# Linear attention, a dense and a sparse mixture of experts in one kernel: a new order for the first unit of tokens, its loads on two queues, small inputs loaded later

## The chip, the cores and the metric

The kernel runs on one core of a Trainium2 chip. The metric is the device time of one execution in microseconds, the median of several runs. A core has TensorE (matmuls, with a separate stream of weight loads), VectorE, ScalarE, GpSimd, and SyncE (SP), which here only issues DMAs. Each engine executes its own instructions in program order and waits on semaphores for the others. DMAs are issued from queues; in this kernel SP's is the main one, ScalarE has one as well. The profile calls the engines PE (PEld for its weight loads), DVE, ACT, POOL and SP.

## The reference

Three parts follow each other. The first is a gated linear attention over 2 batches, 8 heads, 768 tokens and 48 channels per head; the second is a dense mixture of 4 experts on the 1,536 rows of 384 channels, weighted by normalised `domain_probs`; the third a noisy top-2 mixture of 8 experts.

```python
for t in range(S):
    state = alpha[:, :, t, :, None] * state + einsum('bhd,bhe->bhde', k[:, :, t], v[:, :, t])
    y[:, :, t] = einsum('bhd,bhde->bhe', q[:, :, t], state)
...
p = domain_probs / (domain_probs.sum(-1, keepdims=True) + 1e-09)
for e in range(E):
    h = np.maximum(x @ w1[e], 0.0)
    out += p[:, e:e + 1] * (h @ w2[e])
```

The third part takes logits from two small matrices (`w_gate`, `w_noise`) and an input `noise`, and sends each row through its two best experts.

## The kernel before

The attention works on units of 128 or 256 tokens (`sizes`); the first unit has 128. A unit is cut into groups of two blocks, a block being a pair of heads by 128 tokens; the first unit has two groups (k=0 and k=1 in the plan), the second, of 256 tokens, four (k=2 to 5). Each group goes through stages: `decays` (alpha is transposed on TensorE into a "tr" bank; VectorE takes running products forward, A, and backward, F, and a reciprocal `rc`), `keys` (k transposed, VectorE multiplies it by F to K; ScalarE scales it to G), `queries` (q transposed, times A, is Q), `scores` (G by Q on TensorE into banks sc0 and sc1; VectorE masks them to M), `keys_back` (K transposed back, copied by ScalarE to Kn), `states` (Kn by v into sc0; VectorE writes or updates the states S), and `outputs` (S by Q and M by v into sc1; ScalarE copies them to `xn`). At the end of a unit `back` transposes `xn`; ScalarE writes `xh` (for the first unit `x32` ahead of it), VectorE the remainder `xl`.

`plan()` gives every stage of every group a step; `stream()` walks the steps, and inside a step goes by a fixed order of stages. `busy(n)` puts n dummy matmuls of 512 columns ahead of a stage, by the table `IDLE`; fourteen more stand at the start of the program. Every stage takes its bank for dummies from the four "g" banks, whether n is 0 or not. The schedule is manual: what is written first is issued first on each engine.

When `rows_at[0]` steps are done, the first expert of the dense mixture starts on the first 128 tokens: `hidden` for one column of 128 hidden channels at a time (the matmuls of line 475, six records each, into a "g" bank; ScalarE writes `hh`, VectorE `hl`), then the products. `drive` deals its twelve steps out over the steps of the attention that go on beside it, up to the end of the second unit, and ahead of each `W.step` may prepare a piece of weights (line 142 on ScalarE: the four pieces of the first expert's second matrix, numbers 0 to 3; numbers 4 to 7 are its first matrix and are first used as they are).

On SP's queue stand, in this order: the first unit in two halves of the heads (alpha, k, q each, 96 KB), its v, and then, of the second unit and the weights, `"a", "k", "q", 4, 0, 5, "v", 1, 6, 2, 7, 3`. ScalarE's queue has the small inputs `prob`, `noise` and the two halves of `wgn`, which arrive in rows of 16 or 32 bytes. A row of the attention's inputs has 48 numbers, 192 bytes; a unit of 128 tokens has 1,024 rows for each of the four inputs. A first-matrix piece has 384 rows of 1 KB, a second-matrix piece 256 rows of 1.5 KB. Four short operations of VectorE (lines 553 to 556) normalise `prob` ahead of everything else; it is first used in line 521, when the first products are done.

Of the kernel before, what the change touches and what calls it, by code (L numbers as in the profile page):

```python
# [10 lines left out]
F32 = mybir.dt.float32  # L11
# [6 lines left out]
OP = mybir.AluOpType  # L18
AX = mybir.AxisListType

P = 128
# [7 lines left out]
def kernel(  # L29
# [16 lines left out]
    nc = tc.nc  # L46
    B, H, S, D = q.shape
    N, DM = out.shape
    E1, _, FF = moe_w1.shape
    E2 = moe2_w1.shape[0]  # L50
    NB = N // P
# [6 lines left out]
    BM = UM // P  # L58
    KD = DM // P
    KF = FF // P  # L60
    HP = H // 2
# [5 lines left out]
    const = ctx.enter_context(tc.tile_pool(name="const", bufs=1))  # L67
# [5 lines left out]
    def ps(tag, bufs=1):  # L73
        return psum.tile([P, 512], F32, tag=tag, name=tag, bufs=bufs)
# [111 lines left out]
    def busy(n):  # L186

        t = ps("g", 4)
        for _ in range(n):
            nc.tensor.matmul(t.rearrange("x (c i) -> x c i", c=4), ones_b, ones_b[:, None, :].to_broadcast([P, 4, P]),  # L190
                             start=True, stop=True)
# [21 lines left out]
    apool = att.enter_context(tc.tile_pool(name="apool", bufs=1))  # L213
# [4 lines left out]
    for nm, n in (("a", 2), ("k", 1), ("q", 1)):  # L218
        for i in range(n):
            t = apool.tile([P, BM, H, 64], F32, name=f"x_{nm}{i}", tag=f"x_{nm}{i}")  # L220
# [8 lines left out]
    V = {}  # L229

    def inputs(nm, u):
        if nm == "a":
            return X[nm, u % 2]
        return X[nm, 0] if u else early[:, "kq".index(nm)]

    def load_unit(u, names, p0=0, p1=HP):

        if u >= NU:
            return
        b, h0 = divmod(starts[u], S)  # L240
        hs = slice(2 * p0, 2 * p1)
        for nm in names:
            if nm == "v":
                V[u] = apool.tile([P, BM, H, D], F32, tag="v", name="v", bufs=2)
            for c in range(sizes[u] // P):
                frm = src[nm][b, hs, h0 + c * P:h0 + (c + 1) * P, :].rearrange("h p d -> p h d")
                if nm == "v":
                    nc.sync.dma_start(V[u][:, c, hs], frm)
                    continue
                nc.sync.dma_start(inputs(nm, u)[:, c, hs, :D], frm)  # L250


    prob = const.tile([P, NB, E1], F32, name="prob")
    nc.scalar.dma_start(prob, moe_domain_probs.rearrange("(b p) e -> p b e", p=P))
    noise = const.tile([P, NB, E2], F32, name="noise")
    nc.scalar.dma_start(noise, moe2_noise.rearrange("(b p) e -> p b e", p=P))
    wgn = const.tile([P, KD, 2 * E2], F32, name="wgn")
    nc.scalar.dma_start(wgn[:, :, :E2], moe2_w_gate.rearrange("(c p) e -> p c e", p=P))
    nc.scalar.dma_start(wgn[:, :, E2:], moe2_w_noise.rearrange("(c p) e -> p c e", p=P))

    W = Weights()

# [2 lines left out]
    for i in range(2):  # L265
        t = apool.tile([P, UM], F32, name=f"suffix{i}")
# [3 lines left out]
    for p in range(HP):  # L270
        t = apool.tile([P, BM + 1, 2 * D], F32, name=f"S{p}")
# [6 lines left out]
    def attention(u):  # L278

        b, h0 = divmod(starts[u], S)  # L280
# [6 lines left out]
        def slot(c):  # L287
            return (starts[u] // P + c) % (BM + 1)

        def at(i):  # L290
            return slice(i * P, (i + 1) * P)

        def transposed(nm, g):
            t = ps("tr", 2)
            for i, (p, c) in enumerate(groups[g]):
                nc.tensor.transpose(t[:, at(i)], inputs(nm, u)[:, c, 2 * p:2 * p + 2, :].rearrange("x h d -> x (h d)"), ident)  # L296
            return t[:, :UM]
# [19 lines left out]
        def keys(g):  # L317
            A, K, Q, G, rc = st[g]
            nc.vector.tensor_mul(K, transposed("k", g), st[g, "F"])
            for i in range(BM):  # L320
                nc.scalar.activation(G[:, at(i)], K[:, at(i)], AF.Copy, scale=rc[:, i:i + 1])

        def queries(g):
            A, K, Q, G, rc = st[g]
            nc.vector.tensor_mul(Q, transposed("q", g), A)
# [15 lines left out]

        def scores(g):
            A, K, Q, G, rc = st[g]
            t = [ps("sc0"), ps("sc1")]
            for i in range(BM):
                for j in range(2):
                    rows = slice(64 * j, 64 * j + D)
                    nc.tensor.matmul(t[j][:, at(i)], G[rows, at(i)], Q[rows, at(i)], start=True, stop=True)  # L348
            for j in range(2):
                M = apool.tile([P, BM, P], F32, tag=f"M{j}", name="M")  # L350
                nc.vector.tensor_mul(M, t[j][:, :UM].rearrange("x (c i) -> x c i", c=BM),
                                     tri[:, None, :].to_broadcast([P, BM, P]))
                st[g, j] = M

# [22 lines left out]

        def outputs(g):
            A, K, Q, G, rc = st[g]
            t = ps("sc1")  # L380
            for i, (p, c) in enumerate(groups[g]):
                inter = not (first and c == 0)
                if inter:
                    nc.tensor.matmul(t[:, i * 2 * D:(i + 1) * 2 * D], Q[:, at(i)], St[p][:, slot(c), :],  # L384
                                     start=True, stop=False)
                for j in range(2):
                    o = i * 2 * D + j * D
                    nc.tensor.matmul(t[:, o:o + D], st[g, j][:, i, :], V[u][:, c, 2 * p + j, :], start=not inter,  # L388
                                     stop=not inter or j == 1)
            if g == 0:  # L390
                st["xn"] = apool.tile([P, BM, DM], F32, tag="xn", name="xn")
            xn = st["xn"]
            p = groups[g][0][0]
            n = 2 * D * BM // UB
            nc.scalar.activation(xn[:, :UB, 2 * p * D:2 * p * D + n],
                                 t[:, :UB * n].rearrange("x (c d) -> x c d", c=UB), AF.Copy)

        def loads(g, names, v):
            p0, p1 = groups[g][0][0], groups[g][-1][0] + 1
            if p1 % 2 == 0:  # L400
                load_unit(v, names, p1 - 2, p1)
# [22 lines left out]
        def outputs_(g):  # L424
            outputs(g)
            if g == len(groups) - 1:
                load_unit(u + 2, "v")

        return len(groups), UB, (outputs_, states, keys, scores, keys_back, queries_, decays_), back

    suffixes = itertools.cycle(suffix)

    rows_at = {}
    NEAR = 2

    IDLE = {(2, 0): 5, (1, 0): 5, (2, 1): 2, (1, 1): 4, (2, 2): 4, (1, 2): 2, (0, 0): 1, (0, 1): 1, (0, 2): 1}

    def plan():
        at = {}
        base = 0  # L440
        k = 0
        for u in range(NU):
            n, UB, stages, back = attention(u)
            for g in range(n):
                near = k < NEAR
                for order, (stage, off) in enumerate(zip(stages, (5, 4, 1, 3, 3, 2, 0) if near else (7, 6, 1, 5, 3, 2, 0))):
                    at.setdefault(base + off, []).append((order, k, stage, g))
                end = base + (5 if near else 7)
                base += 2 if near else 3
                k += 1  # L450
            for c in range(UB):
                at.setdefault(end + 1 + c, []).append((-1, k, back, c))
            rows_at[u] = end + 1 + UB
        return at

    steps = plan()

    def stream():
        for i in range(max(steps) + 1):
            for order, k, f, g in sorted(steps.get(i, ()), key=lambda z: z[:2]):  # L460
                busy(IDLE.get((order, k), 0))
                f(g)
            yield

# [84 lines left out]
                pass  # L549


    psm = const.tile([P, NB], F32, name="psm")
    nc.vector.reduce_sum(psm, prob, axis=AX.X)
    nc.vector.tensor_scalar(psm, psm, 1e-9, None, op0=OP.add)
    nc.vector.reciprocal(psm, psm)
    nc.vector.tensor_mul(prob, prob, psm[:, :, None].to_broadcast([P, NB, E1]))

    for i in range(2):
        load_unit(0, "akq", i * HP // 2, (i + 1) * HP // 2)
    load_unit(0, "v")  # L560
    for what in ("a", "k", "q", 4, 0, 5, "v", 1, 6, 2, 7, 3):
        if type(what) is int:
            W.fetch(what)
        else:
            load_unit(1, what)
    W.n_raw = 2 * NG
    rows_now = stream()
    now = 0

    def until(i):  # L570
        nonlocal now
        while now < i:
            now += 1
            next(rows_now, None)
            yield

    for _ in until(rows_at[0]):
        if now >= 15 and W.n_prep < 4:
            W.prep()

    def n_moe(n):
        return KF + n // P * (KF // 2)
# [11 lines left out]
    hst = ExitStack()  # L594
    hidden_in.append((hst.enter_context(tc.tile_pool(name="hpool", bufs=1, side="right")), 4 * P))


    NS = E2 * SB
    BL = 3
# [554 lines left out]
```

## Time and profile before

| | us |
|---|---|
| median of 3 runs | 765.06 (764.93 to 765.39) |
| the profiled execution, its own time | 764.46 |
| its span, first to last instruction | 762.7 |
| TensorE busy | 750.6 |
| VectorE busy | 351.4 |
| ScalarE busy | 246.0 |
| GpSimd busy | 160.6 |

The span is what the trace covers; the execution's own time is a little longer. Busy time counts an engine's instructions; what it waited for, and since when, is in the rows further down. Each row of a timeline merges equal instructions that follow each other: start, length, engine, line, operation, output and inputs, shape, how many, and in brackets how long the engine was idle before it and whose semaphore ended that.

### The profile page before, as it was taken

What the parts mean: (1) busy time and instruction counts of PE and PEld (TensorE: products, weight loads), DVE (VectorE), ACT (ScalarE), POOL (GpSimd) and SP (SyncE); (2) the same over time, 40 slices, a digit from 0 to 9 for tenths busy, and PEclk for the clock granted to TensorE, in tenths of its full rate; (3) what the DMA queues carried; (4) which work ended last, traced back from release to release, by engine and by line L of the source; (5) the groups of instructions that cost most, each with busy time, mean ns of one, the idle gap of its engine ahead of it and who ended that gap; (6) DMA issues with size and microseconds to landing.
All of it is one profiled execution on the core that took longest, in us unless ns stands there. A gap on an engine that the chain in (4) does not pass through costs nothing.

```text
span 762.7 us, 11958 instructions
## 1 busy us (share of the span) xinstructions
PE 750.6 (98%) x4658; PEld 707.6 (93%) x4658; DVE 351.4 (46%) x864; ACT 246.0 (32%) x481; POOL 160.6 (21%) x174
## 2 busy tenths in 40 slices
PE   9999999999999999999999999999999999999996
PEld 5899999999998989899899999989999999999996
DVE  5877566663222131222212346366745554654641
ACT  2643322232311031211223323333525444444430
POOL 2520000001510023100124100011352424424331
PEclk9999999999999999999999999999999999999999
DMA  9836212100620012100023300011763554654710
GB/s 187 221 75 125 52 32 43 22 1 8 209 75 1 0 42 83 43 0 1 22 63 103 94 21 12 32 42 29 220 206 122 186 161 148 212 161 136 228 63 32
DMA packets 97998, 66.97 MB, mean 88 GB/s; under 512 B 57577, under 2 KB 94500, under 8 KB 97936
## 3 DMA queue, kind: packets, MB, share of 16 engines
q1 hardware_dynamic: 89008, 51.92, 24.6%
q0 software_dynamic: 5024, 14.13, 5.8%
q8 instruction: 39, 0.64, 0.4%
q10 hardware_dynamic: 3904, 0.10, 0.4%
q14 instruction: 23, 0.19, 0.1%
HBM read 56.69 MB, written 9.82 MB: 87 GB/s over the span
## 4 chain that ended last, share of the span: by engine, by line
PE 93%; DVE 5%; ACT 1%; issue 0%; POOL 0%; POOLq 0%; DVEq 0%
PE g L480 13%; PE g L479 13%; PE g L481 13%; PE g L494 10%; PE g L496 10%; PE g L495 10%; PE g L994 3%; PE g L996 3%; PE g L995 3%; PE sc L388 2%; PE tr L296 2%; PE sc L348 2%; PE tr L927 1%; PE sc L362 1%; PE sc L384 1%; PE g L190 1%
## 5 line engine op out<-in xcount | busy, mean ns | idle before, releaser
L485 ACT ACTIVATE hh<-g 128x384 fp32r<-128x384 f32 (+8 forms) x200 | 96.9, 485 | 281.2 <-PE g L481 261.6
L486 DVE SCALAR_TENSOR_TENSOR hl<-g,hh 128x384 fp32r<-128x384 f32 (+8 forms) x200 | 109.5, 550 | 159.5 <-ACT hh L485 154.1
L494 PE MATMUL g<-w2h,hl 128*128 128x384 f32 x464 | 161.7, 348 | 0.0
L496 PE MATMUL g<-w2h,hh 128*128 128x384 f32 x464 | 156.5, 337 | 0.0
L495 PE MATMUL g<-w2l,hh 128*128 128x384 f32 x464 | 156.4, 337 | 0.0
L479 PE MATMUL g<-xh,w1l 128*128 128x512 f32 (+2 forms) x360 | 127.0, 353 | 0.0
L480 PE MATMUL g<-xl,w1h 128*128 128x512 f32 (+2 forms) x360 | 124.4, 346 | 0.0
L481 PE MATMUL g<-xh,w1h 128*128 128x512 f32 (+2 forms) x360 | 124.3, 345 | 0.0
L143 POOL TENSOR_TENSOR w1l<-raw,w1h 128x768 fp32r<-128x768 f32 x16 | 29.3, 1841 | 280.2 <-ACT w1h L142 280.2
L494 PEld LDWEIGHTS g<-w2h,hl 128*128 128x128 f32 x464 | 87.3, 188 | 0.5
L495 PEld LDWEIGHTS g<-w2l,hh 128*128 128x128 f32 x464 | 87.4, 188 | 0.3
L496 PEld LDWEIGHTS g<-w2h,hh 128*128 128x128 f32 x464 | 87.2, 188 | 0.0
L523 DVE SCALAR_TENSOR_TENSOR acc<-g,prob,acc 128x384 f32<-128x384 f32 x36 | 22.2, 618 | 119.7 <-PE g L496 119.7
L480 PEld LDWEIGHTS g<-xl,w1h 128*128 128x128 f32 x360 | 67.8, 188 | 6.3 <-DVE xl L413 0.3
L481 PEld LDWEIGHTS g<-xh,w1h 128*128 128x128 f32 x360 | 67.7, 188 | 6.3
L479 PEld LDWEIGHTS g<-xh,w1l 128*128 128x128 f32 x360 | 67.8, 188 | 6.0
L479 PE MATMUL g<-xth,w1l 128*128 128x256 f32 (+6 forms) x216 | 73.2, 339 | 0.0
L480 PE MATMUL g<-xtl,w1h 128*128 128x256 f32 (+6 forms) x216 | 71.4, 331 | 0.1
L481 PE MATMUL g<-xth,w1h 128*128 128x256 f32 (+6 forms) x216 | 71.3, 330 | 0.0
L142 ACT ACTIVATE w2h<-raw 128x768 fp32r<-128x768 f32 x44 | 36.4, 843 | 35.3 <-issue 23.0
L945 POOL DMA_INDIRECT out_dram<-yo,si_c x26 | 26.1, 1004 | 87.1 <-DVE yo L944 80.9
L994 PE MATMUL g<-hh,w2l 128*128 128x432 f32 (+4 forms) x120 | 43.3, 361 | 0.0
(193 smaller groups left out, 1056.1 us busy)
## 6 DMA issues: line engine op xcount, KB each, us to landing
raw<-in_moe_w_dram SPq DMA_DIRECT2D x92, 384.0 KB, 4.3
v<-in_v_dram SPq DMA_DIRECT2D x12, 192.0 KB, 2.9
out_dram<-zero SPq DMA_DIRECT2D x1, 2304.0 KB
x2d<-acc SPq DMA_DIRECT2D x12, 192.0 KB, 4.5
x_a<-in_alpha_dram SPq DMA_DIRECT2D x20, 96.0 KB, 2.1
x_k<-in_k_dram SPq DMA_DIRECT2D x18, 96.0 KB, 2.6
x_q<-in_q_dram SPq DMA_DIRECT2D x18, 96.0 KB, 2.7
acc<-in_moe_w_dram SPq DMA_DIRECT2D x4, 384.0 KB, 7.1
```

The costliest lines, as they stand in the source:

```text
L142: nc.scalar.activation(hi, r, AF.Copy)
L143: (nc.gpsimd if e < E1 or own else nc.vector).tensor_sub(lo, r, hi.bitcast(F32))
L479: nc.tensor.matmul(t[:, :n], wl, hx[:, kd, t0:t0 + n], start=(kd == 0), stop=False)
L480: nc.tensor.matmul(t[:, :n], wh, lx[:, kd, t0:t0 + n], start=False, stop=False)
L481: nc.tensor.matmul(t[:, :n], wh, hx[:, kd, t0:t0 + n], start=False, stop=(kd == KD - 1))
L485: nc.scalar.activation(hh[:, :n], t[:, :n], AF.Relu)
L486: nc.vector.scalar_tensor_tensor(hl[:, :n], t[:, :n], 0.0, hh.bitcast(F32)[:, :n], op0=OP.max, op1=OP.subtract)
L494: nc.tensor.matmul(t[:m, :DM], hl[:, o:o + m], wh, start=(f == 0), stop=False)
L495: nc.tensor.matmul(t[:m, :DM], hh[:, o:o + m], wl, start=False, stop=False)
L496: nc.tensor.matmul(t[:m, :DM], hh[:, o:o + m], wh, start=False, stop=(f == KF - 1))
L945: nc.gpsimd.indirect_dma_start(out=parts_of_out[s], out_offset=bass.IndirectOffsetOnAxis(ap=SLOT[e * SB + s][2][:n, e * SB + s:e * SB + s ...
L994: nc.tensor.matmul(t[:, :n], wl, hh[:, :n], start=(f == 0), stop=False)
```

## The change

The first unit gets step tables of its own. All of its transposes of alpha, k and q come first, then both scores, both outputs, `back`, both `keys_back` and both `states`; its rows are ready after step 6 instead of 8, so the expert starts two steps sooner, with the first unit's `states` still to come. From the third group on every stage keeps its step. Two transposes, the second group's scores and its outputs take "g" banks, masks have two buffers each. The dummies are dealt out anew. The first unit's k and q are issued from ScalarE's queue; `prob` follows weight piece 1 on SP's queue, `noise` and `wgn` come on SP's queue after the attention. The normalising of `prob` stands behind step 6. The condition `now >= 15` that goes was never true there.

```diff
-    def load_unit(u, names, p0=0, p1=HP):
+    def load_unit(u, names, p0=0, p1=HP, queue=nc.sync):
...
+    for i in range(2):
+        load_unit(0, "a", i * HP // 2, (i + 1) * HP // 2)
+        load_unit(0, "kq", i * HP // 2, (i + 1) * HP // 2, nc.scalar)
+    load_unit(0, "v")
...
-            t = ps("tr", 2)
+            t = ps("g", 4) if u == 0 and (nm, g) in (("q", 0), ("a", 1)) else ps("tr", 2)
...
-            t = [ps("sc0"), ps("sc1")]
+            t = [ps("g", 4), ps("g", 4)] if u == 0 and g else [ps("sc0"), ps("sc1")]
...
-                M = apool.tile([P, BM, P], F32, tag=f"M{j}", name="M")
+                M = apool.tile([P, BM, P], F32, tag=f"M{j}", name="M", bufs=2)
...
-            t = ps("sc1")
+            t = ps("g", 4) if u == 0 and g else ps("sc1")
...
-    NEAR = 2
-
-    IDLE = {(2, 0): 5, (1, 0): 5, (2, 1): 2, (1, 1): 4, (2, 2): 4, (1, 2): 2, (0, 0): 1, (0, 1): 1, (0, 2): 1}
+    NEAR = ({"decays": 0, "keys": 0, "queries": 0, "scores": 2, "outputs": 4, "keys_back": 6, "states": 7},
+            {"decays": 0, "keys": 1, "queries": 1, "scores": 3, "outputs": 5, "keys_back": 6, "states": 8})
+    FAR = {"decays": 0, "keys": 1, "queries": 2, "keys_back": 3, "scores": 5, "states": 6, "outputs": 7}
+    ORDER = ("outputs", "states", "keys", "scores", "keys_back", "queries", "decays")
+
+    IDLE = {("scores", 0): 5, ("scores", 1): 6, ("outputs", 0): 2, ("outputs", 1): 1, ("back", 1): 2}
...
-    psm = const.tile([P, NB], F32, name="psm")
-    nc.vector.reduce_sum(psm, prob, axis=AX.X)
-    nc.vector.tensor_scalar(psm, psm, 1e-9, None, op0=OP.add)
-    nc.vector.reciprocal(psm, psm)
-    nc.vector.tensor_mul(prob, prob, psm[:, :, None].to_broadcast([P, NB, E1]))
-
-    for i in range(2):
-        load_unit(0, "akq", i * HP // 2, (i + 1) * HP // 2)
-    load_unit(0, "v")
-    for what in ("a", "k", "q", 4, 0, 5, "v", 1, 6, 2, 7, 3):
+    for what in ("a", "k", 4, "q", 5, "v", 6, 7, 0, 1, "p", 2, 3):
         if type(what) is int:
             W.fetch(what)
+        elif what == "p":
+            nc.sync.dma_start(prob, moe_domain_probs.rearrange("(b p) e -> p b e", p=P))
...
     for _ in until(rows_at[0]):
-        if now >= 15 and W.n_prep < 4:
-            W.prep()
+        pass
+
+    psm = const.tile([P, NB], F32, name="psm")
+    nc.vector.reduce_sum(psm, prob, axis=AX.X)
+    nc.vector.tensor_scalar(psm, psm, 1e-9, None, op0=OP.add)
+    nc.vector.reciprocal(psm, psm)
+    nc.vector.tensor_mul(prob, prob, psm[:, :, None].to_broadcast([P, NB, E1]))
```

In `plan()` the groups of `NEAR` take their steps from these tables, and inside a step the first group's keys and queries come behind the other stages, followed by the second group's decays.

## Rows read from the trace of the kernel before

**Rows 1.** The page, TensorE's busy time, share of the span, instructions.

```profile
PE 750.6 (98%) x4658; PEld 707.6 (93%) x4658; DVE 351.4 (46%) x864; ACT 246.0 (32%) x481; POOL 160.6 (21%) x174
```

**Rows 2.** Windows: busy time by engine, granted clock, DMA share, GB/s.

```profile
5.00:30.00 25.00, 23.56 (x176) 17.58 (x175) 18.50 (x63) 10.98 (x29) 6.22 (x4) 1.00 1.01 234
30.00:40.00 10.00, 10.00 (x88) 9.35 (x87) 8.44 (x29) 5.27 (x14) 4.64 (x3) 1.00 0.74 157
```

**Rows 3.** Timeline of TensorE, 0 to 30 us.

```profile
1.13 4.90 PE L190 MATMUL g<-ones_b 128*128 128x512 bf16 x14 [1.13 <-DVE ones_b L185]
5.86 0.38 PE L296 MATMUL tr<-ident,x_a 128*128 128x128 f32 x2
...
9.31 0.72 PE L348 MATMUL sc<-Q,G 48*128 48x128 f32 x8
...
20.23 0.94 PE L475 MATMUL g<-acc,raw 128*128 128x128 f32 x6 [0.34 <-ACT acc L411]
...
29.00 0.69 PE L362 MATMUL sc<-v,Kn 128*128 128x96 f32 x4 [0.39 <-DVE M L351]
```

**Rows 4.** Line 190, the dummies, up to 40 us; durations in ns.

```profile
L190 PE MATMUL g<-ones_b x39: 379/379/634, 1.1 to 25.0; 128*128 128x512 bf16 x39
```

**Rows 5.** Timeline of VectorE, 0 to 31 us.

```profile
4.40 0.20 DVE L553 TENSOR_REDUCE psm<-prob 128x12 f32<-128x48 f32 x1 [2.17 <-DMA prob<-in_moe_domain_probs_dram]
...
5.14 0.21 DVE L556 TENSOR_TENSOR prob<-prob,psm 128x48 f32<-128x48 f32 x1
6.36 0.73 DVE L312 TENSOR_TENSOR_SCAN suffix<-tr,tri 128x127 f32<-128x127 f32 x2 [1.00 <-PE tr L296]
...
13.80 0.72 DVE L312 TENSOR_TENSOR_SCAN suffix<-tr,tri 128x127 f32<-128x127 f32 x2
...
15.27 0.40 DVE L319 TENSOR_TENSOR K<-tr,suffix 128x256 f32<-128x256 f32 x1
15.69 0.76 DVE L351 TENSOR_TENSOR M<-sc,tri 128x256 f32<-128x256 f32 x2
17.51 0.86 DVE L372 COPY S<-sc 48x48 f32<-48x48 f32 x4 [1.07 <-PE tr L296]
18.41 0.42 DVE L325 TENSOR_TENSOR Q<-tr,A 128x256 f32<-128x256 f32 x1
...
20.93 0.56 DVE L413 TENSOR_TENSOR xl<-g,xh 128x384 fp32r<-128x384 f32 x1
...
22.74 0.29 DVE L486 SCALAR_TENSOR_TENSOR hl<-g,hh 128x128 fp32r<-128x128 f32 x1 [0.92 <-ACT hh L485]
...
24.14 1.15 DVE L374 SCALAR_TENSOR_TENSOR S<-S,A,sc 48x48 f32<-48x48 f32 x4
```

**Rows 6.** Timeline of ScalarE, 0 to 30 us.

```profile
8.27 0.69 ACT L321 ACTIVATE G<-K,rc 128x128 f32<-128x128 f32 x2 [2.71 <-DVE K L319]
...
19.69 0.49 ACT L411 ACTIVATE acc<-g 128x384 f32<-128x384 f32 x1 [0.29 <-PE g L407]
...
26.23 0.84 ACT L142 ACTIVATE w2h<-acc 128x768 fp32r<-128x768 f32 x1 [0.71 <-DMA acc<-in_moe_w_dram]
```

**Rows 7.** Waits of SP's queue, 0 to 60 us: in total, times, longest.

```profile
SPq L250 <- DMA prob<-in_moe_domain_probs_dram: 1.5, 1, 1.5
SPq L248 <- DMA noise<-in_moe_noise_dram: 1.0, 1, 1.0
```

**Rows 8.** DMA views of 0:22, 20:22 and 7:8 (q1 SP, q10 ScalarE; share of engines).

```profile
DMA packets 18198, 4.46 MB, mean 203 GB/s; under 512 B 16510, under 2 KB 18198, under 8 KB 18198
...
q1 hardware_dynamic: 14294, 4.37, 87.8%
q10 hardware_dynamic: 3904, 0.10, 12.5%
...
DMA packets 619, 0.71 MB, mean 355 GB/s; under 512 B 30, under 2 KB 619, under 8 KB 619
...
q1 hardware_dynamic: 487, 0.09, 60.2%
```

## Prediction before the run

> **What bounds the kernel.** The page comes first: the span is 762.7 us and TensorE is busy for 750.6 us of it [rows 1], so almost every microsecond of TensorE work or idleness shows in the total. The change touches the head only, so next come windows: from 5 to 30 us TensorE is busy for 23.56 of 25 us, and from 30 to 40 us for 10.00 of 10 [rows 2]. Past 30 us, then, whatever the head is late or early by is carried to the end; nothing later waits for a fixed moment. Inside the head the TensorE timeline [rows 3] shows fourteen dummies from 1.13 us, the first transposes behind them at 5.86, the first scores at 9.31, the first expert matmul at 20.23, and at 29.00 the `states` matmuls of the fourth group (k=3), which waited 0.39 us for a mask product of VectorE. That last row is my yardstick: up to there VectorE's chain sets the pace, behind it TensorE is full. The VectorE timeline [rows 5] gives the price of each step, ScalarE's the hops between [rows 6], the DMA views the loads [rows 7, 8].
>
> The profiled run took 764.46 us, 1.76 above its span and 0.60 below the median of the runs, 765.06. I add differences worked out in the span to the median. 0.2% is 1.53 us, about what a measurement of this kernel can tell from no change.
>
> **Dummies.** Before, 39 stand in the trace [rows 4]: 14 at the start and 25 from the table `IDLE`. The new table has 5+6+2+1+2 = 16. Nine fewer, 512 columns each at 2.4 GHz = 0.213 us, take 1.9 us of TensorE work away. That is worth something only where the dummies did not fill a wait.
>
> **First loads on two queues.** SP stood still twice, 1.5 us for `prob` and 1.0 us for `noise`, before it issued k's and q's second halves and v [rows 7]. That goes, and the first loads no longer share the engines with 3,904 small packets. But TensorE is held by its fourteen dummies until 5.86 in either order, and no row there shows a transpose waiting for a load; I price this at 0. Without that cover it would be worth at most the 2.5 us that SP stood still.
>
> **The new order of the first unit**, by durations of before [rows 5, 6], with 6.36 as VectorE's start as now. Decays take 1.5 us, keys 0.35, queries 0.4: both groups' six steps follow each other without a gap and end at 6.36 + 2 x 2.3 = 11.0. Scores 0 are masked by 11.7; G of group 1 is ready at 10.6 + 0.7 = 11.3, its scores at 12.2, its masks at 12.9. Outputs (0.82 us each) with transposes and dummies between run from 12.6 to 14.8, `xn` is copied by 15.3, turned by 15.8. ScalarE has G of the third group first (0.7), then `x32` and `xh` (0.4 each): 17.2. VectorE's `xl` follows at 17.8 and the queries of the third group, whose transposes wait for a PSUM buffer of `keys_back`, by 18.4. The expert's first matmul comes at about 17.9 instead of 20.23 [rows 3], but two `states` with their copies, a `keys_back`, a decays and a keys step, done by then before, are still to do. The five extra PSUM buffers and second mask buffers remove waits already counted here as absent; they cost nothing, as no engine executes an allocation.
>
> **The moved sum of `prob`.** The four operations that normalise `prob` ran from 4.40 to 5.35 [rows 5], while VectorE had nothing else to do. Now they stand in VectorE's program order behind all steps above: 0.95 us on the path. Much more, they wait for `prob`, now the twenty-second load, behind eleven others of the second unit and the weights on SP's queue. VectorE executes in program order, so behind them wait `hl`, the state copies, every later decays; and TensorE waits for these: the second `states` needs the bank that the first copies release.
>
> **When does `prob` land?** By 22.0 us SP's queue had moved 14,294 packets; 18,198 - 16,510 = 1,688 of these are weights, and all 12,288 rows (192 bytes each) of the first two units are in [rows 8]. In the new order six weight loads stand before `prob`: four first matrices of 384 rows and two second ones of 256, 2,048 packets. The 360 missing ones take 1.2 us at the 589 per 2 us of 20 to 22 us: 23.2. Off come the small packets, 12.5% of 22 us of all engines = 2.75 us, and 0.4 us for the stretch from 7 to 8 us in which the queue ran at 0.60 [rows 8]; on comes `prob`'s own share, 1,536 of packets of which 3,904 took 2.75 us: 1.1 us. That gives 21.2 us. Bounds: if all 2.5 us of SP's standing come back in place of 0.4, 19.1; and if completion lags as that of the third weight piece did, whose 1,920 weight packets had landed only at 26.2 [rows 6], then 26.2 - 2.75 + 0.4 + 1.1 = 24.9. I take 21.2, from the packet counts, since one late completion may be one slow engine.
>
> **The sum.** From `prob`'s landing VectorE does, until the mask half that frees the fourth group's `states`: normalising 0.95; five `hl` of 0.2; two state copies of 0.86; two decays of 1.5; two keys of 0.4; masks 0.7 and 0.37; one queries 0.35; one state update 1.15: 10.0 us, and about 0.6 in two hops over TensorE (scores between copies and masks), 10.6 in all [rows 5]. So that `states` starts at landing + 10.6, against 29.00 before [rows 3]. By then TensorE has done one more expert column (six matmuls, 0.67 us), since the expert's work is now spread over sixteen steps of the stream instead of fourteen: five columns ahead of this `states` instead of four. Net: landing + 10.6 - 29.0 - 0.67 = landing - 19.1. With 21.2 this is +2.1 us, **767.2**; with the bounds 0.0 and +5.8. Were `prob` there at 18.4 the sum would be -0.7.
>
> The later weights cost no more: ScalarE's wait for the third piece, 0.71 us before [rows 6], comes back at about 25 us, while VectorE is the late one. The late loads of `noise` and gate weights are needed hundreds of us later, and SP's queue is mostly empty in between: 0.
>
> **The clock.** The stall leaves TensorE without work from about 20.2 (second expert column done, second `states` blocked) to 23.2, three us, where the longest gap of before in this stretch was well under one and the clock column says 1.00 throughout [rows 2]. The fourteen dummies at the start took 4.90 us [rows 3] where fourteen times 0.213 is 2.98: TensorE, idle before, ran part of them at the lower of its two levels, 1.2 GHz (the column prints 1.00 there too, so it has to be read from the durations), and lost 1.9 us. A fall in the stall would cost about as much; the sum takes none, for no row shows a fall after a gap. The Trainium skill (TensorE: Matmul & The Clock Gate, Part 1) says that an idle array is put back to half rate and released only by sustained work; by that rule the sum would be +4.0 us in place of +2.1. The start of this trace agrees with the release; no stretch of it shows a fall.
>
> **Rivals.**
> 1. *The other side: TensorE's sum decides.* `prob` lands before VectorE gets to it (about 18.4), and the new order lets VectorE run without gaps. Then the nine dummies are the gain: 765.06 - 1.9 = **763.2**. For it: before, VectorE idles inside the first unit, 1.07 us ahead of the second group's state copies alone [rows 5]. Against: 2.75 us off the queue don't bring 23.2 below 18.4, and VectorE's steps are the same in number. It decides from a landing of 18.4 down.
> 2. *A wash:* `prob` lands at 19.1 to 20.6, the stall is as long as what the order saves: **765.6**, up to 766.5. For it: two queues may start sooner than I count.
> 3. *The stall and a fallen clock:* 767.2 + 1.9 = **769.1**.
> 4. *Late completion* as of that weight piece: landing 24, **770.0**.
>
> **How the numbers follow.** Forecast (landing 20.7 to 22.8) 0.38; late or fallen clock, 0.18 together; wash 0.22; TensorE's sum 0.22. Slower by over 0.2% is then 0.56, within 0.22, faster 0.22. The likeliest's own range is 766.7 to 768.8. For 8 in 10: the low end is TensorE's sum, 763.2, leaving out its better half (0.1); the high end takes in the fallen clock, 769.3, leaving out most of the late completion (0.09).
>
> **What would show it.** VectorE's first reduction of `prob` at 21 to 22 us with an idle time of 2 to 4 us before it, released by the DMA; the first scores still near 9.3; the first expert matmul near 18; a TensorE gap of 2 to 3 us behind the second expert column, put down to VectorE's copies; the yardstick `states` near 32 instead of 29; TensorE full behind it. I am wrong if the reduction doesn't wait: then the packet count misled me, and the order's own gain is seen bare; or if TensorE fills the stall with work that I counted as blocked.

## The result and the profile after

The changed kernel takes 773.37 us (median of 4 runs, 772.59 to 773.77) where the kernel before took 764.99 beside it: a ratio of 1.0109 [1.0092, 1.0127], 8.4 us slower. The forecast was 767.2, at most 769.3. The direction and the place were right, the change is four times the one forecast.

The page, TensorE's line, against [rows 1]: 1.3 us more of busy time, and the span grew from 762.7 to 771.7 us.

```profile
span 771.7 us, 11935 instructions
PE 751.9 (97%) x4649; PEld 709.0 (92%) x4649; DVE 353.8 (46%) x864; ACT 247.1 (32%) x481; POOL 160.5 (21%) x174
```

TensorE's timeline of the changed kernel, against [rows 3] (start, duration, line, operation; in brackets the idle time ahead and what ended it):

```profile
18.84 0.83 PE L486 MATMUL g<-acc,raw 128*128 128x128 f32 x6
...
26.79 1.14 PE L363 MATMUL sc<-v,Kn 128*128 128x96 f32 x4 [5.59 <-DVE S L373]
...
37.65 0.69 PE L363 MATMUL sc<-v,Kn 128*128 128x96 f32 x4 [0.38 <-DVE M L352]
```

The yardstick, `states` of the fourth group, moved from 29.00 to 37.65: 8.65 us, about what the whole kernel lost (8.4). Nearly everything happens ahead of it, and most of it in one gap: TensorE waits 5.59 us for VectorE's state copies. VectorE's timeline of the same kernel shows what holds them, and GpSimd's, behind it, who was at work meanwhile:

```profile
19.04 0.42 DVE L326 TENSOR_TENSOR Q<-tr,A 128x256 f32<-128x256 f32 x1 [0.21 <-PE tr L297]
23.11 0.20 DVE L585 TENSOR_REDUCE psm<-prob 128x12 f32<-128x48 f32 x1 [3.65 <-DMA prob<-in_moe_domain_probs_dram]
23.35 1.81 DVE L586 TENSOR_SCALAR psm<-psm 128x12 f32<-128x12 f32 x1
25.20 0.23 DVE L587 RECIPROCAL psm<-psm 128x12 f32<-128x12 f32 x1
25.46 0.21 DVE L588 TENSOR_TENSOR prob<-prob,psm 128x48 f32<-128x48 f32 x1
25.59 0.28 DVE L497 SCALAR_TENSOR_TENSOR hl<-g,hh 128x128 fp32r<-128x128 f32 x1
25.79 0.85 DVE L373 COPY S<-sc 48x48 f32<-48x48 f32 x4
...
30.57 0.29 DVE L497 SCALAR_TENSOR_TENSOR hl<-g,hh 128x128 fp32r<-128x128 f32 x1 [0.92 <-ACT hh L496]
```

```profile
21.57 3.56 POOL L143 TENSOR_TENSOR w2l<-acc,w2h 128x768 fp32r<-128x768 f32 x2 [16.75 <-ACT w2h L142]
```

The reduction waits 3.65 us for `prob`'s transfer, as forecast, but it lands at 23.1. Then an addition on twelve elements a partition takes 1.81 us where its neighbours take 0.2: it ends when GpSimd's second subtraction of that pair ends (21.57 + 3.56 = 25.13). The windows of the changed kernel (stretch; busy time of TensorE, weight load, VectorE, ScalarE, GpSimd; granted clock, DMA share, GB/s) answer [rows 2]:

```profile
15.00:20.00 5.00, 3.74 (x33) 3.30 (x32) 2.70 (x8) 2.61 (x8) 0.00 (x0) 1.00 0.97 293
20.00:25.00 5.00, 1.20 (x11) 1.00 (x9) 1.85 (x2) 2.13 (x4) 3.43 (x2) 0.81 1.12 276
25.00:30.00 5.00, 3.21 (x16) 3.02 (x18) 4.40 (x19) 0.32 (x2) 0.14 (x1) 0.50 0.26 50
30.00:35.00 5.00, 5.00 (x35) 4.49 (x33) 3.71 (x12) 2.54 (x7) 1.81 (x1) 0.66 0.75 144
```

From 20 to 25 us TensorE is busy for 1.20 us, and then its clock stands at 0.50, the lower level of 1.2 GHz, until past 30. Six expert matmuls that take 0.83 us at 18.84 take 1.49 in that stretch.

So there are three suspects in the stall (the transfer, GpSimd, the clock) and one outside it (the order itself, which I had at -0.7 us). The experiments take them one by one. Each ratio is against runs of the kernel before on the same chip, whose median was 764.7 to 764.8 throughout.

### The profile page after: what moved, and what is told of

It reads as the page before. It is cut to its first block, busy times and chain, and to the rows that moved or that the text cites. A ratio compares the mean times of both kernels' runs of the same rounds, so it can differ in the third digit from the quotient of the medians.

```text
span 771.7 us, 11935 instructions
## 1 busy us (share of the span) xinstructions
PE 751.9 (97%) x4649; PEld 709.0 (92%) x4649; DVE 353.8 (46%) x864; ACT 247.1 (32%) x481; POOL 160.5 (21%) x174
## 4 chain that ended last, share of the span: by engine, by line
PE 91%; DVE 4%; SPq 2%; DMA 1%; ACT 1%; issue 0%; POOL 0%; POOLq 0%; DVEq 0%
PE g L491 13%; PE g L490 13%; PE g L492 13%; PE g L505 10%; PE g L507 10%; PE g L506 10%; PE g L1007 3%; PE g L1009 3%; PE g L1008 3%; PE sc L389 2%; PE tr L297 2%; PE sc L349 2%; PE sc L363 1%; PE tr L940 1%; PE sc L385 1%; PE sc L665 1%
```

## The experiments

### Without the wait for `prob`: e1_late_norm, e2_prob_first

```
# e1: the four operations leave their place ahead of the first phase; in moe1:
+        if e == 0 and t0 == 0:
+            normalise()        # behind the 8 hidden columns, ahead of the products
# e2: prob first on SP's queue behind the first unit
-    for what in ("a", "k", 4, "q", 5, "v", 6, 7, 0, 1, "p", 2, 3):
+    for what in ("p", "a", "k", 4, "q", 5, "v", 6, 7, 0, 1, 2, 3):
```

> The changed kernel, with the four operations that normalise prob moved behind the eight hidden columns of the first 128 tokens, just ahead of their first use; loads and order as in the changed kernel. Theory A (the wait for prob holds VectorE, and what else was lost hangs on it): the wait is gone, TensorE's gap of 5.6 us and the half clock with it; the fourth group's states start at about 28.5 to 29.5 us, and the time is 764.3 us (763.3 to 765.3), where before is 765.0. Rival B (the expert started two steps earlier outruns its weights and VectorE's copies): a gap of over 2 us stays in front of the second states or behind it, ScalarE waits for the third weight piece until 24 to 25 us, and the time stays above 768.

> The changed kernel, with prob issued on SP's queue behind the first unit's v and ahead of the whole second unit, in place of behind weight piece 1; the normalising where the changed kernel has it. Theory A: prob lands before 12 us, the first reduction doesn't wait, the 0.95 us of normalising stand on VectorE's path at about 19.5 us, outside GpSimd's work: 765.2 us (764.3 to 766.3). Rival B: above 768, as in the other run.

e1: 767.36 (12 runs, 765.49 to 771.52), 1.0033 [1.0020, 1.0045]. e2: 771.00 (4 runs, 767.75 to 771.13), 1.0064 [1.0044, 1.0084]. e1 lies between its two expectations. Moving four small operations gives 6.0 of the 8.4 us back; the wait for `prob` with what hangs on it is the main loss. e2 shows that an earlier place on SP's queue is no cure: three of its four runs took 771.0 to 771.1 at a mean granted clock of 0.993 to 0.994, the fourth 767.75 at 0.999. ScalarE's and TensorE's timelines of e2, a run of 771.00:

```profile
23.59 0.84 ACT L142 ACTIVATE w2h<-acc 128x768 fp32r<-128x768 f32 x1 [4.58 <-DMA acc<-in_moe_w_dram]
24.34 0.36 ACT L340 ACTIVATE Kn<-tr 128x256 f32<-128x256 f32 x1
```

```profile
24.75 0.69 PE L297 MATMUL tr<-ident,x_k 128*128 128x128 f32 x2 [3.68 <-ACT Kn L340]
```

VectorE normalises at 18.40 without a wait, and now the pieces of the second expert matrix, behind `prob` on the same queue, come late. ScalarE too works in program order: its split `w2h` waits 4.58 us, `Kn` stands behind it, and TensorE's next transposes wait for the PSUM bank that `Kn` reads. e1's slowest run shows the same chain, shorter (2.65 and 1.92 us). A second wall stood right behind the first.

### Half of the change each: k_order_only, k_loads_only

```
# k_order_only: the changed kernel (plan, dummies, PSUM buffers) with the loads of before
-    for i in range(2):
-        load_unit(0, "a", ...)                  # SP
-        load_unit(0, "kq", ..., nc.scalar)
+    nc.scalar.dma_start(prob, ...); nc.scalar.dma_start(noise, ...)   # and wgn
+    # normalising of prob, then load_unit(0, "akq", ...), all ahead of the stream
+    for what in ("a", "k", "q", 4, 0, 5, "v", 1, 6, 2, 7, 3):
# k_loads_only: the kernel before (plan, dummies) with the reverse of these lines,
#   and normalise() placed as in e1
```

> The new order of the first unit alone: step tables, dummies, extra banks and mask buffers as in the changed kernel; all loads, the small inputs and the normalising as before. If the order by itself is worth nothing or little (my sum without a wait was -0.7 us, and the start of the dummies varies by as much): 764.5 us (763.5 to 766). If the order needs the quicker loads, TensorE waits for the first unit's second half (k's second half was issued at 4.39 us): 766 to 767.

> The loads alone, in the order of before: first unit on two queues, small inputs later, second unit and weights in the changed kernel's order; the normalising just ahead of its first use. My sum has nothing for the quicker first loads, as fourteen dummies cover them: 765.0 us (764.3 to 765.5). Rival: the wait for the third weight piece (0.71 us before) goes and VectorE loses 0.95 us of work it had no use for: 764.0.

k_loads_only: 764.91 (11 runs), 0.9999 [0.9991, 1.0008]. The loads on two queues are worth nothing, as priced. k_order_only: 767.75 (6 runs), 1.0040 [1.0027, 1.0052]. The order alone, with the loads of before, loses 2.9 us where I had it gaining 0.7. Its windows and two lines of TensorE's timeline:

```profile
20.00:25.00 5.00, 3.53 (x31) 2.85 (x28) 3.90 (x18) 2.84 (x8) 3.49 (x2) 1.00 0.99 320
25.00:30.00 5.00, 4.61 (x27) 4.61 (x28) 3.77 (x14) 2.08 (x4) 2.63 (x3) 0.66 1.03 235
```

```profile
23.49 0.71 PE L349 MATMUL sc<-Q,G 48*128 48x128 f32 x8 [1.01 <-DVE S L373]
...
25.39 0.69 PE L363 MATMUL sc<-v,Kn 128*128 128x96 f32 x4 [0.82 <-DVE M L352]
```

No gap is much over 1 us, yet the clock falls behind a stretch in which TensorE was busy for 3.53 of 5 us; the kernel before, busy for 4.64 there, kept it at 1.00.

### GpSimd: e4_no_add

```
-    nc.vector.tensor_scalar(psm, psm, 1e-9, None, op0=OP.add)
```

The kernel leaves out the 1e-9 in the divisor of `prob`.

> The changed kernel without the second of the four normalising operations (it leaves out the addition of 1e-9 to the sums). That operation took 1.81 us in place of 0.21, and ended when GpSimd's subtraction of a weight piece ended. If that one form of operation is what waits for GpSimd: the other three take 0.2 us each, the states come 1.8 us sooner, 771.6 us. If any of VectorE's operations on SBUF waits there: the reciprocal or the product takes 1.6 us or more in its place, 773.2.

771.94 (4 runs), 1.0090 [1.0073, 1.0107]: 1.4 us under the changed kernel, with intervals that overlap. VectorE's and GpSimd's timelines of its slowest run (774.67):

```profile
23.88 0.23 DVE L586 RECIPROCAL psm<-psm 128x12 f32<-128x12 f32 x1
24.14 0.25 DVE L587 TENSOR_TENSOR prob<-prob,psm 128x48 f32<-128x48 f32 x1
```

```profile
22.52 3.57 POOL L143 TENSOR_TENSOR w2l<-acc,w2h 128x768 fp32r<-128x768 f32 x2 [17.68 <-ACT w2h L142]
```

By this run alone only the addition would wait for GpSimd. But VectorE's product of `prob` ended at 24.39, where GpSimd's first operation had just ended (half of 3.57 behind 22.52: 24.31), so it may have been lucky; f5 below shows that it was.

### The clock: e3_dummies_in_stall, f5_stall_filled

```
# entries added to IDLE of the changed kernel
# e3:  ("states", 1): 22
# f5:  ("states", 1): 22, ("queries", 2): 5, ("scores", 2): 4, ("states", 2): 3
```

> The changed kernel with 22 more dummies (4.7 us at 2.4 GHz) ahead of the second group's states, where TensorE stood idle for 5.6 us. If the fallen clock is a part of the loss: the clock column stays at 1.00, the states matmuls behind the stall take 0.58 us in place of 1.14, the fourth group's states start 2 to 2.5 us sooner than 37.65, and the time is 771.0 us (770.3 to 771.6) against 773.4. If VectorE's chain sets the pace there whatever the clock: 773.0 to 774.

> The changed kernel with 34 more dummy products on TensorE: 22 ahead of the states of the third group, which stand behind the wait for prob, 5 ahead of its queries, 4 ahead of its scores, 3 ahead of the states of the fourth group. It leaves out nothing. Theory (the wait costs its stall and, on top, a fallen clock that fillers all the way through take away): about 770.5 us, that is 2 to 3.5 us under the changed kernel, granted clock 1.00 from 10 to 40 us. Rival (the fall of the clock only runs beside idle time and costs nothing of its own): 773.4, as the changed kernel, whatever the clock.

e3: 774.20 (4 runs, 770.45 to 775.66), 1.0106 [1.0079, 1.0133], not the 771.0 expected. In its profiled run (775.66) the clock held through the stall, and fell behind it: TensorE was busy for 3.16 us of 25 to 30, and the granted clock was 0.50 from 30 to 35 and 0.56 from 35 to 40. The fall was only put off, and cost as much later. One of its four runs took 770.45 at a mean granted clock of 0.998; the others had 0.991 to 0.994 and took 3.7 to 5.2 us more. What kept the clock up in that one isn't shown. f5 fills that stretch too: granted clock 1.00 in every window from 10 to 50 us, 771.73 (6 runs), 1.0096 [1.0078, 1.0114], 1.6 us under the changed kernel (the intervals overlap). Its yardstick stands at 36.30 against 37.65, 1.35 us earlier, but only 0.8 of that is the clock: 0.53 us came from VectorE, which was through with the normalising sooner (`hl` at 25.06 against 25.59). Behind that `hl` the changed kernel's VectorE waited for TensorE at 32.50 (0.60 us) and 35.63 (0.20), and f5's did not. With the clock held, the wait for `prob` is still worth 771.73 - 766.98 = 4.75 us against f1 below. VectorE's timeline of f5, with GpSimd's pair running from 21.5 to 25.1:

```profile
22.84 0.20 DVE L585 TENSOR_REDUCE psm<-prob 128x12 f32<-128x48 f32 x1 [4.01 <-DMA prob<-in_moe_domain_probs_dram]
23.07 0.26 DVE L586 TENSOR_SCALAR psm<-psm 128x12 f32<-128x12 f32 x1
23.37 0.23 DVE L587 RECIPROCAL psm<-psm 128x12 f32<-128x12 f32 x1
23.63 1.50 DVE L588 TENSOR_TENSOR prob<-prob,psm 128x48 f32<-128x48 f32 x1
25.06 0.28 DVE L497 SCALAR_TENSOR_TENSOR hl<-g,hh 128x128 fp32r<-128x128 f32 x1
```

Here it is the product that lasts until GpSimd's second operation ends, while the addition slipped into the end of the first (23.3). Reduction and reciprocal keep 0.20 and 0.23 us inside GpSimd's work. So the addition and the product each last until the GpSimd operation that they meet has ended; how much of its time is left over is chance. Other runs bear the addition out: it took 1.47 us in e3, 0.65 in e1, f1 and f4, 0.64 in f3 and 0.45 in g2, each time up to within 0.04 us of the end of a GpSimd subtraction, and 0.17 in e2 and k_loads_only, where none ran. The Trainium skill (SBUF — State Buffer, Who interferes with whom) says that VectorE and GpSimd share a port pair as an exclusive lock for a whole instruction, and that two SBUF inputs are enough for VectorE to need it against a GpSimd operation that reads SBUF; the trace agrees for the product (1.50 us). For the addition, which has one such input, the same section names operations in a two-port mode; its 1.81 us fit that, but no run here shows the mode.

### What the order costs with the clock held: f1, f2, f3, f4

Fillers are dummy matmuls that keep TensorE busy through a gap.

```
# f1_late_norm_filled: e1, IDLE +
+  ("queries", 2): 5, ("keys", 3): 7, ("scores", 2): 1, ("states", 2): 2
# f2_order_filled: k_order_only, IDLE +
+  ("queries", 2): 5, ("scores", 2): 4, ("states", 2): 3
# f3_late_norm_weights: e1, the weight pieces nearer to their places of before, prob last
-    for what in ("a", "k", 4, "q", 5, "v", 6, 7, 0, 1, "p", 2, 3):
+    for what in ("a", "k", 4, "q", 0, "v", 5, 1, 6, 2, 7, 3, "p"):
# f4_both: f3 with the 12 dummies of f2
```

> The kernel with the late normalising and 15 more dummies, put where its TensorE stood idle: 5 ahead of the third group's queries, 7 ahead of the fourth group's keys, 1 and 2 ahead of the third group's scores and states. That kernel took 767.4 us, its clock column fell to 0.50 from 24 to 37 us, and its ScalarE waited 2.65 us for the first weight piece. Theory C (a thin TensorE from 15 to 25 us lets the clock fall, and that is the loss): the column stays at 1.00 and the time is 765.0 us (764.2 to 766.0). Rival W (ScalarE's wait for the weight piece, which holds the turned keys, is the loss): 766.5 to 768.

> The new order alone (loads and normalising as before) with 12 more dummies in its gaps: 5 ahead of the third group's queries, 4 and 3 ahead of the third group's scores and states. Without them it took 767.75 us with the clock at 0.50 from 26 to 29 us. Theory C: the column stays at 1.00, 765.3 us (764.5 to 766.2). If the order loses by its waits and not by the clock: 767.3 or more.

> The kernel with the late normalising, with the queue behind the first unit in another order: alpha, k, piece 4, q, 0, v, 5, 1, 6, 2, 7, 3, and prob last. No dummies added. Rival W: ScalarE no longer waits over 1 us for a weight piece, 765.2 us. Theory C: the stretch from 15 to 25 us is still thin and the clock still falls, 766.3 to 767.5.

> Both: late normalising, weight pieces 0 and 1 earlier, prob last, and 12 dummies in the gaps (5 ahead of the third group's queries, 4 and 3 ahead of its scores and states). Theory C and rival W together leave the order's own sum, which I put at -0.7 us: 764.3 us (763.4 to 765.2), the fourth group's states at 28 to 29 us.

f1 766.98 (10 runs), 1.0025 [1.0015, 1.0034]; f2 766.99 (11), 1.0026 [1.0017, 1.0035]; f3 767.60 (7), 1.0038 [1.0023, 1.0052]; f4 766.74 (11), 1.0021 [1.0012, 1.0030]. Where fillers hold the clock (1.00 in every window of f1, f2 and f4 from 5 to 50 us), all three agree on about 2 us, whatever the loads, the weights and `prob` do; the expectation that only the clock was left (764.3 to 765.3) is wrong. This is the order's own price: in f4, TensorE, VectorE and ScalarE wait for no transfer up to its yardstick, at 31.19 against 29.00. Fillers gain 0.4 (e1 to f1) to 0.9 us (f3 to f4), each with overlapping intervals. f3's weights gain nothing on their own. VectorE's and ScalarE's timelines of f4, one round of a group:

```profile
24.93 0.29 DVE L497 SCALAR_TENSOR_TENSOR hl<-g,hh 128x128 fp32r<-128x128 f32 x1 [0.92 <-ACT hh L496]
...
29.18 0.41 DVE L320 TENSOR_TENSOR K<-tr,suffix 128x256 f32<-128x256 f32 x1
30.51 0.29 DVE L497 SCALAR_TENSOR_TENSOR hl<-g,hh 128x128 fp32r<-128x128 f32 x1 [0.92 <-ACT hh L496]
30.72 0.75 DVE L352 TENSOR_TENSOR M<-sc,tri 128x256 f32<-128x256 f32 x2
```

```profile
29.62 0.69 ACT L322 ACTIVATE G<-K,rc 128x128 f32<-128x128 f32 x2 [0.59 <-DVE K L320]
30.22 0.26 ACT L496 ACTIVATE hh<-g 128x128 fp32r<-128x128 f32 x1
```

VectorE writes `K`; ScalarE makes `G` of it, and only then `hh`, whose column was done earlier; VectorE's `hl` waits for `hh`, and the masks, which free the next `states`, stand behind `hl`. That costs 0.92 us of VectorE in a round, and a round takes 5.58 us (24.93 to 30.51). The kernel before has the same wait [rows 5] and the same pitch, 23.41 to 29.00 between the `states` of the third and fourth group; there three expert columns fell into that round (`hl` at 23.94, 26.80 and 28.32), here two, one having been done earlier.

So this wait can't be what the new order lost against the old: up to the yardstick both have it twice. The rows in which VectorE waited tell the two apart. First the kernel before (beside 17.51 and 22.74 of [rows 5]), then f4 up to 20 us:

```profile
12.56 0.86 DVE L372 COPY S<-sc 48x48 f32<-48x48 f32 x4 [1.18 <-PE sc L362]
...
19.36 0.73 DVE L312 TENSOR_TENSOR_SCAN suffix<-tr,tri 128x127 f32<-128x127 f32 x2 [0.53 <-PE tr L296]
...
28.32 0.29 DVE L486 SCALAR_TENSOR_TENSOR hl<-g,hh 128x128 fp32r<-128x128 f32 x1 [0.92 <-ACT hh L485]
```

```profile
13.19 0.76 DVE L352 TENSOR_TENSOR M<-g,tri 128x256 f32<-128x256 f32 x2 [1.18 <-PE g L349]
14.79 0.73 DVE L313 TENSOR_TENSOR_SCAN suffix<-tr,tri 128x127 f32<-128x127 f32 x2 [0.85 <-PE tr L297]
...
18.19 0.56 DVE L414 TENSOR_TENSOR xl<-g,xh 128x384 fp32r<-128x384 f32 x1 [1.51 <-ACT xh L413]
...
19.94 0.29 DVE L497 SCALAR_TENSOR_TENSOR hl<-g,hh 128x128 fp32r<-128x128 f32 x1 [0.55 <-ACT hh L496]
```

With 0.21 us more at 18.96, f4's VectorE waits 4.30 us ahead of 20 us, the kernel before 2.78 (1.18, 1.07, 0.53). From VectorE's start on the first unit to the yardstick before takes 22.64 us and f4 24.18: the 1.54 between them are these 1.52 us of waits, the longest of them for `xh`, which ScalarE copies once the first unit is done. In this run VectorE also started 0.65 us later (7.01 against 6.36).

### The hop taken out: g1_before_late_hl, g2_both_late_hl

```
     def hidden(e, f, hx, lx, t0, n, H_):
+        pay()                       # the hl owed by the column before
         t = ps("g", 4)
...
-        nc.vector.scalar_tensor_tensor(hl[:, :n], ...)
+        owed.append(low) if e == 0 and t0 == 0 else low()
```

> The kernel before with one edit: in the first phase of the first expert, VectorE's subtraction hl of a hidden column is issued ahead of the next column in place of right behind its own, so that the steps of the units stand ahead of it in VectorE's order. It leaves out nothing. Theory (hl waits for ScalarE's hh, which stands behind the exponential there, and only matters where VectorE sets the pace; in this order TensorE is full behind 30 us): 764.3 to 765.0, no gain that can be told. Rival (VectorE's wait for hh sets the pace in both orders): 0.9 us a round over three rounds, some 762.5.

> f4_both (the new order, prob's normalising behind the hidden columns, the weight pieces as before, fillers) with hl issued ahead of the next column. It leaves out nothing. Theory (in the new order VectorE's chain sets the pace of the rounds, and 0.9 us of each is its wait for hh, which stands behind G on ScalarE): 764.0 to 765.4, against 766.74 of f4_both, and the states of the fourth group at 29 to 30 us, against 31.2. Rival (what the new order loses lies in its first 20 us, in the two columns that VectorE does early and the later start, and not in the rounds): 766.7, as f4_both.

g2: 764.97 (11 runs), 1.0006 [0.9997, 1.0015], against 766.74 of f4: 1.8 us from nothing but VectorE's program order. `states` of the third to fifth group, TensorE's timeline of g2:

```profile
25.09 0.58 PE L363 MATMUL sc<-v,Kn 128*128 128x96 f32 x4
...
30.12 0.69 PE L363 MATMUL sc<-v,Kn 128*128 128x96 f32 x4
...
35.25 0.69 PE L363 MATMUL sc<-v,Kn 128*128 128x96 f32 x4
```

The pitch is 5.03 and 5.13 us in place of 5.58, and no wait stands ahead of these. It shrinks by less than 0.92 because the masks now wait 0.47 us for the scores. g1: 763.72 (11 runs), 0.9987 [0.9979, 0.9996]: 1.0 us better than the kernel before, between the two expectations. The same hop set part of the pace there, mostly ahead of 30 us: counted from VectorE's start on the first unit the yardstick comes at 22.00 us in place of 22.64, the `states` two rounds later at 32.85 in place of 33.68. (The operation of ScalarE that `hh` stands behind is the scaling of K to G, not an exponential.) g1 is the fastest of all kernels here, 9.6 us under the changed one.

With the hop out of both, the new order is still 1.25 us behind the old (g2 against g1), with it 1.9 (f4 against before). So by the medians the hop makes 0.7 of the new order's loss. By the traces the rest lies in VectorE's waits ahead of 20 us, as g2's rival had it; no run takes those out.

## Why the prediction missed

Right were the mechanism (the reduction of `prob` in VectorE's order, waiting 3.65 us for the DMA where 2 to 4 were forecast, TensorE held by the state copies, though for 5.59 us and not 2 to 3), the loads at 0 and the yardstick, which carried nearly all of the loss. The first expert matmul came at 18.84 against 17.9, the first scores at 10.47 against 9.3: VectorE started 0.7 us later in this run. That start moves from one profiled run to the next (5.97 in e1), and behind a wait for a transfer it doesn't count.

The sum was landing - 19.1 and gave +2.1. Five of its terms were too small, and the two largest errors are the landing and the normalising:

- **Landing** 21.2, measured 23.1: +1.9. 14,167 small packets had moved by 22.0 (14,191 by 23.0), above the 13,824 of units and `prob` by which I counted, and 2,190 others, above the 2,048 weight packets; so the count was about right for the bulk, and `prob` was complete only 1.1 us behind it. That is half of the late completion that I had turned down as one slow engine's; which packet came last isn't shown. e4 and f5 had 23.6 and 22.8. (Ahead of `prob` the trace has fourteen issues of the second unit and the weights, not eleven; the count of packets had them all.)
- **Normalising** 0.95, measured 2.56: +1.6, until GpSimd's operation ended. My duration was right for [rows 5], where GpSimd was through with zeroing S at 4.82; at the new place it splits weights.
- **Hops** behind the landing 0.6, measured two of 0.92 for `hh` alone (1.8 in the changed kernel's and f5's waits): about +1.2. One stood in [rows 5], and I took it as that row's and not as each round's.
- **The column done early** -0.67, measured 0: with two columns in a round in place of three the pitch stays 5.58, and TensorE waits 0.59 us ahead of f4's `states` where it waited 0.39. That the nine dummies gave nothing for the same reason is argued and not tested.
- **The clock** 0 in the sum, 1.9 in a rival: it fell, and cost 0.8 us at the yardstick, the two waits for TensorE that f5 doesn't have; the medians differ by 1.6, not clear of noise. I left it out of the sum because no row of before showed a fall. The rule of the Trainium skill weighed there (TensorE: Matmul & The Clock Gate, Part 1) agrees with this trace: TensorE stopped at about 21 us, and the granted clock was 0.50 from 24 to 33.

Together 2.1 + 1.9 + 1.6 + 1.2 + 0.7 + 0.8 = 8.3, against 8.65 at the yardstick and 8.4 in the medians. VectorE's own steps behind the normalising make up the rest: they took 9.4 us, and the list of the sum has 9.05.

The step that was wrong in its reading, and not only in size, is "were `prob` there at 18.4 the sum would be -0.7". In f1, f2 and f4 VectorE waits for no transfer from its start on the first unit to the yardstick, and they measured about +2. The -0.7 even holds 0.95 of normalising that in these three stands elsewhere, so by the sum they should come out at -1.6. At f4's yardstick (+2.2) the gap of 3.8 is made up of the waits for `hh` (0.55, 0.92 and 0.92 against 0.6: 1.8), the column (0.7), VectorE's later start (0.65), the queries of the third group, done 12.4 us behind that start and not 12.0 (0.3), and VectorE's own steps (0.35). The old order pays the 0.92 twice as well; against it the new one lost mainly by VectorE's longer waits ahead of 20 us, as above. The row of `hl` in [rows 5] and the 5.59 us from one `states` to the next could have told of the wait that repeats.

Rival 1 (TensorE's sum, 763.2) was given 0.22. The fastest kernel with the new order, g2, took 764.97, and in f4, where `prob` holds nothing up, VectorE's waits set the yardstick all the same.

## What to carry to other kernels

An operation moved to a later place in an engine's order needs three looks at the new place: what it waits for there, who else is at work there (a VectorE operation of 0.2 us took 1.8 beside GpSimd), and what queues behind it. Look for the small wait that repeats in every round, and take it out: here that gave 1.0 us in the old order and 1.8 in the new. Before it is called the reason for a difference between two orders, look whether both have it. When a stall was filled here to hold the clock, the stretch behind it had to be filled as well.

## What the runs showed of the hardware that I had not expected

- A VectorE addition of 128x12 elements took 0.21 us in [rows 5]'s place and 1.81 beside GpSimd's 128x768 subtractions, the 128x48 product 0.21 and 1.50; reduction and reciprocal, on the same tiles, were not touched (0.20 and 0.23 in f5).
- TensorE's clock fell to its lower level with gaps no longer than 1.3 us (k_order_only, busy for 3.53 of 5 us), and stayed there while TensorE was busy: in e1's profiled run it was 0.50 from 25 to 35 us with 4.72 and 5.00 us of each five busy.
